# First batch's feed-forward in eight plain block products; the sums of weight blocks made during the second batch

## The chip, the cores and the metric

One core of a Trainium2 chip. The metric is the device time of one execution in microseconds (us); lower is better. The engines named below are PE (TensorE, matrix products), DVE (VectorE), ACT (ScalarE), POOL (GpSimd) and SP (the queue from which most DMAs are issued).

## The reference

Eight batches of attention over 576 positions (8 heads of 64, a window of 128 keys, a bias by distance), and behind it a feed-forward part with a maximum over three products:

```python
scores = scale * np.matmul(q, k.transpose(0, 1, 3, 2))
...
mask = (rel >= 0) & (rel < window)
scores = np.where(mask, scores + bias[None], -1000000000.0)
...
attn = attn / (np.sum(attn, axis=-1, keepdims=True) + 1e-09)
return np.matmul(attn, v).astype(np.float32)
...
h = np.maximum(np.maximum(x @ w1, x @ w2), x @ w3)
return (h @ w_out).astype(np.float32)
```

x has 4608 rows (8 batches of 576) of 512; w1, w2, w3 are 512x768, w_out is 768x512. The weights come as 64-bit floating-point numbers and are turned into 32-bit words on the chip.

## The kernel before

**Stages.** The program works in stages, one per batch of attention (20 steps each: 4 head pairs of 5 blocks of up to 128 queries). Stage 0 has only the attention of batch 0. Stage 1 has the attention of batch 1 and the feed-forward part of batch 0, stage 2 that of batch 2 beside the feed-forward part of batch 1, and so on; the last stage has only a feed-forward part. Each event (a step's scores, its transposes, a feed-forward unit) has a time number, and events are emitted in the order of these numbers. Within stages 0 and 1 a scheduler may then reorder the instructions of every engine by its own model; from an event early in stage 2 on, PE keeps the program's order (`fix`, `keep_in_program_order`). DVE, ACT, POOL and SP take their instructions in the order in which the scheduler placed them.

**The feed-forward part, seven products.** It is cut into 11 groups per batch: 9 of the first layer (3 blocks of hidden units for each of w1, w2, w3) and 2 of the output. Weights, inputs and outputs of a group are each seen as 2x2 blocks. Instead of the 8 block products of a 2x2 matrix product, each group has 7 "units" (a Strassen scheme in Winograd's form): unit k multiplies a sum of weight blocks by a sum of input blocks. `factors_x` makes the 7 input factors out of the attention's output `xk` (4 differences L397 and 7 splits), `factors_h` those of the hidden activations. Every float32 factor is split into a high part in PE's reduced format and a rest (ACT copy L393, subtraction on DVE or POOL L394), and a unit runs 3 matrix instructions per 128 rows of contraction: 6 in the first layer, 9 in the output layer, each 128x128 by 128x288 (`unit`, L518). The products land in three PSUM banks in turn; `put` (L467 to L484) takes them out, adds the partial sums and takes the maximum over the three weights; L527 copies a partial sum out with ACT.

**The weights.** `preparing` is a generator of 120 steps, 10 for each of 12 weight groups (9 of the first layer, 3 of w_out). `fetch` brings 64-bit words from HBM into two buffers; `convert` (L136 to L144: 2 ACT and 3 DVE operations of 128x512 per buffer) makes float32; `sums` (L158: 4 DVE operations of 128x256) makes the sums of blocks in place; `part` (L168 on ACT, L169 on DVE, 7 times 128x256) splits each of the seven factors into high part and rest. For a first-layer group, the split factors go into two ring tiles `wt0` (4 factors) and `wt1` (3 factors), two of each, and from there to HBM (`keep`, L171). w_out's factors stay in `ow`. The steps are taken two per attention step in stage 0 and two per unit in stage 1 (`weights`). From batch 1 on, the ring is filled from `keep` by DMAs issued on POOL's queue (`stream`, L221), as soon as PE has finished the group two before.

## Time and profile before

Median 839.39 us of 3 runs (836.74 to 843.86).

| what | value |
|---|---|
| span of the profiled execution (first to last instruction) | 837.3 us |
| its own time | not given apart from the span; the span lies inside the range of the runs, 2.1 us under their median |
| PE busy | 770.6 us (92%) |
| DVE, ACT, POOL busy | 560.9, 541.1, 303.7 us |
| mean granted TensorE clock | 0.963 |
| HBM read, written | 157.68 MB, 25.95 MB |
| first feed-forward product of batch 0 | 75.58 us |
| last output product of batch 0 | about 206 us |
| last output product of batch 1 | about 302 us |

The last three rows divide the span: 0 to 75.6 us is stage 0, 75.6 to 206 us is called stage 1 below and 206 to 302 us stage 2. A stage of the middle part (302 to 394 us, 394 to 486 us) takes 92 us. A busy share of an engine says little by itself here: what matters is which engine is full in which stage, and whether PE, which sets the pace from 206 us on, waits for it.

### The profile page before, as it was taken

The page shows a single profiled execution, that of the slowest core. Times are in us where ns is not written, and L with a number is a line of the kernel's source. Part 1 is how long each engine was busy: PE and PEld are TensorE (multiplying, and loading weights), DVE is VectorE, ACT ScalarE, POOL GpSimd, SP SyncE. Part 2 cuts the span into 40 slices and gives each one's busy share as a digit, 9 for nine tenths or more (in the row PEclk, how much of TensorE's full clock was granted, in tenths as well). Part 3 has the DMA queues.
Part 4 walks back from the last instruction along what each step waited for, and adds up shares of the span by engine and source line. Part 5 has one row for each costly group of instructions (what it writes and reads, how often), then busy time and mean ns, then how long its engine had stood idle before and what let it go on. Part 6 is the DMA issues. An engine that isn't in the chain of part 4 may idle for free.

```text
span 837.3 us, 17958 instructions
## 1 busy us (share of the span) xinstructions
PE 770.6 (92%) x6272; PEld 673.2 (80%) x6272; DVE 560.9 (67%) x1830; ACT 541.1 (65%) x1790; POOL 303.7 (36%) x544
## 2 busy tenths in 40 slices
PE   4876777799999999999999999999999999999888
PEld 2434666688988898889988998899888988899887
DVE  5788989987576846677566945675656846572552
ACT  6889888776657666576666755676557656652332
POOL 1221132423256415443255415441345315541431
PEclk9865988899999999999999999999999999999999
DMA  6652667674687747874588648873687557765851
GB/s 234 247 185 82 218 232 271 217 248 162 198 288 256 251 138 251 271 263 166 195 284 281 213 156 277 270 265 128 240 287 251 199 198 233 253 208 165 292 197 56
DMA packets 43401, 184.78 MB, mean 221 GB/s; under 512 B 4784, under 2 KB 13744, under 8 KB 34096
## 3 DMA queue, kind: packets, MB, share of 16 engines
q0 software_dynamic: 18144, 115.61, 41.7%
q1 hardware_dynamic: 25024, 67.97, 22.8%
q8 instruction: 49, 0.80, 0.4%
q14 instruction: 40, 0.33, 0.1%
q10 hardware_dynamic: 144, 0.07, 0.0%
HBM read 157.68 MB, written 25.95 MB: 219 GB/s over the span
## 4 chain that ended last, share of the span: by engine, by line
PE 63%; DVE 12%; issue 9%; POOL 7%; ACT 5%; DMA 3%; SPq 0%; POOLq 0%; DVEq 0%; ACTq 0%
PE ps_m L518 47%; PE ps_x L367 6%; PE ps_s L265 5%; POOL hs L394 5%; PE pt L327 4%; DMA wt<-keep 2%; DVE t L481 1%; DVE wt L169 1%; ACT p L299 1%; POOL pp L345 1%; DVE hq L482 1%; POOL pp L341 1%; DVE hs L144 1%; DVE xs L394 1%; DVE hs L158 1%
## 5 line engine op out<-in xcount | busy, mean ns | idle before, releaser
L518 PE MATMUL ps_m<-xs,wt 128*128 128x288 f32 x3024 | 441.0, 302 | 23.7 <-DVE hq L484 9.3
L518 PEld LDWEIGHTS ps_m<-xs,wt 128*128 128x128 f32 x3024 | 416.0, 192 | 35.8 <-DVE hq L484 11.5
L341 POOL TENSOR_SCALAR_AFFINE_SELECT pp<-pr 128x256 f32<-128x256 f32 (+1 forms) x128 | 54.5, 426 | 278.1 <-ACT pr L340 147.6
L527 ACT COPY t<-ps_m 128x288 f32<-128x288 f32 x264 | 102.1, 392 | 79.0 <-PE ps_m L518 78.9
L518 PE MATMUL ps_m<-hs,ow 128*128 128x288 f32 x1008 | 143.1, 298 | 4.1 <-POOL hs L394 2.4
L518 PEld LDWEIGHTS ps_m<-hs,ow 128*128 128x128 f32 x1008 | 136.0, 188 | 7.0 <-POOL hs L394 3.3
L299 ACT ACTIVATE p<-s,st 128x128 f32<-128x128 f32 (+1 forms) x320 | 127.0, 400 | 18.3 <-DVE st L295 17.4
L394 POOL TENSOR_TENSOR hs<-hq,hs 128x288 fp32r<-128x288 f32 x112 | 95.5, 861 | 100.0 <-ACT hs L393 99.9
L318 ACT ACTIVATE p<-p,st 128x128 f32<-128x128 f32 (+1 forms) x320 | 109.2, 395 | 16.1 <-DVE st L311 16.1
L221 POOL DMA_DIRECT2D wt<-keep x126 | 69.8, 554 | 124.3 <-PE ps_m L518 123.8
L481 DVE TENSOR_TENSOR t<-ps_m,t 128x288 f32<-128x288 f32 x144 | 64.6, 452 | 44.6 <-PE ps_m L518 28.5
L295 DVE CUSTOM_DVE_ANT_0 s<-ps_s,bias 128x128 f32<-128x128 f32 (+1 forms) x300 | 76.6, 281 | 18.5 <-PE ps_s L265 13.7
L367 PE MATMUL ps_x<-pp,v 128*64 128x256 f32 (+3 forms) x768 | 83.2, 341 | 5.2 <-POOL pp L341 4.4
L265 PE MATMUL ps_s<-qk 64*64 64x192 f32 (+1 forms) x1080 | 73.5, 345 | 12.3 <-DVE st L295 7.8
L283 DVE COPY_PREDICATED ps_s<-prev,ps_s 128x256 f32<-128x256 uint8 x120 | 50.7, 422 | 48.8 <-PE ps_s L265 47.4
L327 PE MATMUL pt<-ident,p 128*128 128x128 f32 (+1 forms) x320 | 63.6, 302 | 17.1 <-ACT p L318 15.6
L327 PEld LDWEIGHTS pt<-ident,p 128*128 128x128 f32 (+1 forms) x320 | 36.1, 147 | 49.8 <-ACT p L318 21.5
L367 PEld LDWEIGHTS ps_x<-pp,v 128*64 128x64 f32 (+1 forms) x768 | 46.2, 142 | 32.7 <-issue 10.3
L393 ACT CAST hs<-hq 128x288 fp32r<-128x288 f32 x120 | 49.5, 430 | 35.1 <-DVE hq L482 23.4
L482 DVE TENSOR_TENSOR hq<-t,hq 128x288 f32<-128x288 f32 x144 | 69.5, 486 | 2.8
L265 PEld LDWEIGHTS ps_s<-qk 64*64 64x64 f32 x1080 | 42.4, 141 | 30.6 <-issue 10.8
L340 ACT COPY pr<-pt 128x256 f32<-128x256 f32 x64 | 19.0, 322 | 72.4 <-PE pt L327 72.3
(56 smaller groups left out, 750.2 us busy)
## 6 DMA issues: line engine op xcount, KB each, us to landing
wt<-keep POOLq DMA_DIRECT2D x63, 1024.0 KB, 7.4
wt<-keep POOLq DMA_DIRECT2D x63, 768.0 KB, 4.8
qk<-in_qk SPq DMA_DIRECT2D x31, 576.0 KB, 6.0
hs<-in_w_all SPq DMA_DIRECT2D x24, 512.0 KB, 6.1
v<-in_v SPq DMA_DIRECT2D x32, 320.0 KB, 5.4
keep<-wt SPq DMA_DIRECT2D x9, 1024.0 KB, 4.3
outT<-t SPq DMA_DIRECT2D x64, 144.0 KB, 1.8
keep<-wt SPq DMA_DIRECT2D x9, 768.0 KB, 5.1
```

Source lines behind the costliest of these rows:

```text
L221: nc.gpsimd.dma_start(wts[n, a], keep[n % 9][a])
L265: pe(nc.tensor.matmul(ps[j][d:d + D, o:o + k1 - k0], lhsT=qkt[t][j * D:(j + 1) * D, 0, q0:q0 + D], rhs=qkt[t][j * D:(j + 1) * D, 1, k0:k1] ...
L295: nc.vector.tensor_tensor_reduce(out=s[:n], in0=ps[j][:n, P:2 * P], in1=(bias if i else bias0)[:n, 2 * hp + j, :], scale=-0.125, scalar=3. ...
L299: nc.scalar.activation(p[:n, j], s[:n], AF.Exp, bias=st[:n, 0, a, j:j + 1], scale=-1.0, accum_out=st[:n, 1, a, j:j + 1])
L318: nc.scalar.activation(p[:n, j], p[:n, j], AF.Copy, scale=st[:n, 2, a, j:j + 1])
L327: pe(nc.tensor.transpose(out=pt[:, a, j, :n], in_=p[:n, j], identity=ident[:n, :n]))
L367: pe(nc.tensor.matmul(x[j * D:(j + 1) * D, c:c + e - a], lhsT=vv[:n, i, j * D:(j + 1) * D], rhs=w[:n, j].rearrange("p a b -> p (a b)")[:, ...
L394: e.tensor_tensor(out=lo, in0=src, in1=hi.bitcast(F32), op=ALU.subtract)
L481: nc.vector.tensor_tensor(out=s, in0=ps, in1=e, op=ALU.add)
L482: nc.vector.tensor_tensor(out=h, in0=s, in1=h, op=ALU.max)
L518: pe(nc.tensor.matmul(ps, lhsT=lt, rhs=rt, start=i == 0 and k in (0, 1, 4), stop=i == len(pairs) - 1, skip_group_check=True,))
L527: nc.scalar.copy(out=e, in_=ps)
```

## The change

Batch 0 no longer uses the seven-product scheme. Its groups run in 8 plain block products (`plain_unit`: 4 output blocks, each the sum of two products that are accumulated in one PSUM bank). `plain_x` splits the 4 input blocks as they are, `plain_h` the 4 blocks of each hidden part; there are no differences to make, and `put` gets a finished block, so that it copies (ACT) or takes the maximum (DVE) and adds nothing.

The weights for this are the four blocks themselves: `part` now splits two blocks of 256 in one operation of 128x512. `convert` writes the float32 words densely, and SP sends them to HBM (`w32`). Three of the four split blocks are factors of the seven-product scheme too and go to `keep` at once. The 48 steps of this first pass are taken one per attention step in stage 0 and one per two units in stage 1. A second pass of 36 steps (`add`, `add_part`) makes the rest while batch 1's units run: for each group it reads the float32 words back, places the ring tiles for batch 1, loads the finished factors from `keep`, makes the four sums on DVE, splits them (one operation of 128x768 and one of 128x256 for a first-layer group, four of 128x256 for a group of w_out) and writes them to `keep`. All these DMAs are on SP's queue. A group of the second pass may start when PE's units of the group two before are emitted; w_out's three groups stand between groups 2 and 3. POOL's loads of `keep` begin with batch 2 instead of batch 1.

```diff
     def convert(g, j):
-        lw, hw = words(g, j)
+        both = raws[g, j].rearrange("p (n w) -> p n w", w=2)
+        lw, hw = both[:, :, 0], both[:, :, 1]
...
-        nc.vector.tensor_tensor(out=lf, in0=lf, in1=hw, op=ALU.mult)
...
+        out = raws[g, j][:, :DM].bitcast(F32)
+        nc.vector.tensor_tensor(out=out, in0=lf, in1=hw, op=ALU.mult)
+        nc.sync.dma_start(w32[g][:, j], out)
+
+    def halve(hi, lo, src):
+        nc.scalar.copy(out=hi, in_=src)
+        nc.vector.tensor_tensor(out=lo, in0=src, in1=hi.bitcast(F32), op=ALU.subtract)
...
+        halve(t[:, :, 0], t[:, :, 1], src.rearrange("p (i w) -> p i w", w=W))
+        for i in range(2):
+            plain[g, i, c] = t[:, i]
+            k = SLOT[i, c]
+            if k != 1:
+                nc.sync.dma_start(keep[g][k // 4][:, k % 4], t[:, i].bitcast(F32))
...
+    def add(g):
+        r = hs_p.tile([P, 2, 2 * W], F32, name="hs2", bufs=4)
+        q = sums[g] = hs_p.tile([P, 4, W], F32, name="hs2", bufs=4)
+        nc.sync.dma_start(r, w32[g])
...
+        if g < 9:
+            for a, ks in enumerate(((0,), (0, 2))):
+                place(9 + g, a)
+                for k in ks:
+                    nc.sync.dma_start(wts[9 + g, a][:, k].bitcast(F32), keep[g][a][:, k])
...
+    def add_part(g, a):
+        q = sums[g]
         if g < 9:
-            if k in (0, 4):
-                place(g, k // 4)
-            t = wts[g, k // 4][:, k % 4]
+            t, src = (wts[9 + g, 1][:, 1:2], q[:, 3:]) if a else (wts[9 + g, 0][:, 1:], q[:, :3])
+            halve(t[:, :, 0], t[:, :, 1], src)
+            if a:
+                nc.sync.dma_start(keep[g][1][:, 1:2], t.bitcast(F32))
+            else:
+                nc.sync.dma_start(keep[g][0][:, 1:], t.bitcast(F32))
...
-    g_order = [0, 1, 9, 10, 11, 2, 3, 4, 5, 6, 7, 8]
+        return (n - RING, 6 if a else 3) in used
+
+    A_ORDER = [0, 1, 2, 9, 10, 11, 3, 4, 5, 6, 7, 8]
+    B_ORDER = [0, 1, 2, 9, 10, 11, 3, 4, 5, 6, 7, 8]
...
-    streamed = 18
+    streamed = 36
...
+    def plain_unit(v):
...
+        weights(r % 2, 4 * (A_ORDER.index(g) + 1) if g < 9 else 48)
...
+        if c == 0:
+            part_of["plain"] = ps_m.tile([P, 512], F32, name=f"ps_m{(4 * g + o) % 3}")[:, :C]
+        ps = part_of["plain"]
+        for m, (lt, rt) in enumerate(pairs):
+            pe(nc.tensor.matmul(
+                ps, lhsT=lt, rhs=rt, start=m == 0 and c == 0, stop=m == len(pairs) - 1, skip_group_check=True,
+            ))
...
+        if c:
+            put(0, g, ij, ps, None, u)
...
+        if b == 1:
+            weights(k % 2, 48 + 3 * (B_ORDER.index(g) + 1) if g < 9 else STEPS)
...
     for s in range(1, n_steps + LAG_X):
-        at(s + 0.2, weights, 2)
+        at(s + 0.2, weights, 1)
```

DVE's instructions before, in stage 1 while batch 0's third group is multiplied (hs2_1120 and hs2_1122 hold the weights of first-layer group 4, wt0_1341 its factors, hq the hidden activations, ps_m a PSUM bank):

```order
L137 SCALAR_TENSOR_TENSOR hs2_1122<-hs2_1122 128x512
L158 TENSOR_TENSOR hs2_1120<-hs2_1120 128x256
L141 TENSOR_SCALAR hs2_1122<-hs2_1122 128x512
L481 TENSOR_TENSOR t_1328<-ps_m1_1321,t_1214 128x288
L144 TENSOR_TENSOR hs2_1122<-hs2_1122 128x512
L482 TENSOR_TENSOR hq_1016<-t_1328,hq_1016 128x288
L158 TENSOR_TENSOR hs2_1120<-hs2_1120,hs2_1122 128x256
L397 TENSOR_TENSOR t_1331<-hq_1000,hq_1016 128x288
L158 TENSOR_TENSOR hs2_1122<-hs2_1120 128x256
```

DVE's instructions now, at the same weight group (hs2_924 and hs2_926 hold it, wt0_1177 its four split blocks):

```order
L148 TENSOR_TENSOR hs2_926<-hs2_926 128x512
L544 TENSOR_TENSOR hq_1030<-ps_m1_1139,hq_1030 128x288
L357 TENSOR_SCALAR st_1057<-st_1057 128x4
L344 ISA s_1171,st_1170<-ps_s_105,bias_114 128x128
L344 ISA st_1170 128x1
L360 RECIPROCAL st_1057<-st_1057 128x4
L344 ISA s_1174,st_1170<-ps_s_105,bias_114 128x128
L344 ISA st_1170 128x1
L153 TENSOR_TENSOR wt0_1177<-hs2_924,wt0_1177 128x2x256
L544 TENSOR_TENSOR hq_940<-ps_m2_1161,hq_940 128x288
L153 TENSOR_TENSOR wt0_1177<-hs2_926,wt0_1177 128x2x256
L544 TENSOR_TENSOR hq_961<-ps_m0_1192,hq_961 128x288
```

The four sums and the pairs of addition and maximum are gone from this place; two wide subtractions and single maxima stand there, between the attention's operations (L344 to L360).

DVE's instructions now, in stage 2 while batch 1's second group of products leaves PSUM (hs2_2823 and hs2_2824 are words and sums of w_out's third group, ow its factors, wt1_2588 the ring tile of first-layer group 2). In the program before, this place has no weight work, only the additions and maxima of `put` and the attention's operations:

```order
L153 TENSOR_TENSOR ow5_123<-hs2_2809,ow5_123 128x256
L360 RECIPROCAL st_2556<-st_2556 64x2
L195 TENSOR_TENSOR hs2_2824<-hs2_2823 128x256 x2
L195 TENSOR_TENSOR hs2_2824<-hs2_2824,hs2_2823 128x256
L195 TENSOR_TENSOR hs2_2824<-hs2_2823,hs2_2824 128x256
L549 TENSOR_TENSOR t_2601<-ps_m1_2543,t_2581 128x288
L549 TENSOR_TENSOR t_2613<-ps_m2_2606,t_2539 128x288
L550 TENSOR_TENSOR hq_2482<-t_2601,hq_2482 128x288
L550 TENSOR_TENSOR hq_2491<-t_2613,hq_2491 128x288
L153 TENSOR_TENSOR wt1_2588<-hs2_2584,wt1_2588 128x256
L153 TENSOR_TENSOR ow1_119<-hs2_2824,ow1_119 128x256
L153 TENSOR_TENSOR ow2_120<-hs2_2824,ow2_120 128x256
```

The work of w_out's three groups and of first-layer groups 2 and 3 stands on DVE ahead of the factors that batch 1's fourth group of products needs.

SP's queue now, at the same place (w32 are the float32 words, keep the factors in HBM, v and qk the attention's inputs):

```order
L183 DMA hs2_2808<-w32_10_153 128x1024
L537 DMA outT<-t_2432 128x288
L190 DMA wt0_2586<-keep2_0_129 128x512
L183 DMA hs2_2823<-w32_11_154 128x1024
L288 DMA qk_2370<-in_qk 128x1152
L205 DMA keep2_0_129<-wt0_2586 128x1536
L190 DMA wt1_2588<-keep2_1_130 128x512 x2
L183 DMA hs2_2838<-w32_3_146 128x1024
L293 DMA v_2541<-in_v 128x640
```

Reads of words, loads and stores of factors, and the attention's loads share one queue here; before, it held only outT, qk and v.

More of the change, by code (lines that the diff above doesn't have):

```diff
@@ L119, in attention_maxout_kernel @@
     keep = [[dram.tile([P, e, 2, W], F32, name=f"keep{g}_{a}") for a, e in enumerate((4, 3))] for g in range(9)]
+    w32 = [dram.tile([P, 2, 2 * W], F32, name=f"w32_{g}") for g in range(NG)]
     wts = {}
@@ L189, in preparing @@
                 yield
-            sums(g)
-            yield
-            for k in range(7):
-                while g < 9 and not ahead(g, k // 4):
-                    yield True
-                part(g, k)
+            while 3 <= g < 9 and (g - 3, "plain") not in used:
+                yield True
+            for c in range(2):
+                part(g, c)
                 yield
             if n + 2 < NG:
-                fetch(g_order[n + 2])
+                fetch(A_ORDER[n + 2])
+        for g in B_ORDER:
+            while g < 2 and (8, "plain") not in used:
+                yield True
+            while 2 <= g < 9 and not ahead(9 + g, 1):
+                yield True
+            while g >= 9 and (10, "plain") not in used:
+                yield True
+            add(g)
+            yield
+            for a in range(2):
+                add_part(g, a)
+                yield
+    STEPS = 7 * NG
     prepared = 0
@@ L218, in stream @@
         n, a = divmod(streamed, 2)
-        if n < 9 * B and prepared == 120 and ahead(n, a):
+        if n < 9 * B and prepared == STEPS and ahead(n, a):
             place(n, a)
@@ L485, in put @@
         if w == 2:
-            factors_h(b, p, ij, when + 1)
+            if b:
+                factors_h(b, p, ij, when + 1)
+            else:
+                plain_h(p, ij, when + 1)
     part_of = {}
+    def plain_unit(v):
+        u = v * 77 / 88
+        while todo and todo[0][0] <= u:
+            _, what, args = todo.pop(0)
+            what(*args)
+        g, r = divmod(v, 8)
+        o, c = divmod(r, 2)
+        i, j = ij = ((0, 0), (0, 1), (1, 0), (1, 1))[o]
+        weights(r % 2, 4 * (A_ORDER.index(g) + 1) if g < 9 else 48)
+        if g < 9:
+            wt, x = plain[g, i, c], xs[0, 2 * c + j]
+            pairs = [
+                (wt[:, a, kt * P:(kt + 1) * P], x[:, e, kt]) for kt in range(2) for a, e in ((0, 1), (1, 0), (0, 0))
+            ]
+        else:
+            ms = slice((g - 9) * P, (g - 8) * P)
+            pairs = [
+                (plain[9 + p, i, c][:, a, ms], hs[0, 2 * c + j, p][:, e])
+                for p in range(3) for a, e in ((0, 1), (1, 0), (0, 0))
+            ]
+        if c == 0:
+            part_of["plain"] = ps_m.tile([P, 512], F32, name=f"ps_m{(4 * g + o) % 3}")[:, :C]
[4 more added lines that the diff above has]
+            ))
+        if r == 7:
+            used.add((g, "plain"))
+        if c:
+            put(0, g, ij, ps, None, u)
     def unit(u):
@@ L499, in unit @@
         b, g = divmod(n, 11)
+        if b == 0:
+            return
+        if b == 1:
+            weights(k % 2, 48 + 3 * (B_ORDER.index(g) + 1) if g < 9 else STEPS)
         if g < 9:
             at = b * 9 + g
[L502 to L503 removed]
             wt, x = wts[at, k // 4][:, k % 4], xs[b, k]
@@ L565, in attention_maxout_kernel @@
         if b == 0:
-            at(when, factors_x, 0, 0, 0)
+            at(when, plain_x)
+        if b == 0:
+            pace = (ready[1] - when) / 72
+            for y in range(88):
+                if y == 72:
+                    when = max(when, ready[1])
+                    at(when, factors_x, 1, 63, 1.2)
+                at(when, plain_unit, y)
+                when += pace if y < 72 else O_PACE
+            continue
         pace = (ready[b + 1] - when) / 63 if b + 1 < B else O_PACE
```

68 lines of the change are left out of this document (43 added, 25 removed).

## The prediction

> **What bounds the kernel now.** First I read the slices of the page, to see in which stage which engine is full:
>
> ```profile
> PE   4876777799999999999999999999999999999888
> DVE  5788989987576846677566945675656846572552
> ACT  6889888776657666576666755676557656652332
> PEclk9865988899999999999999999999999999999999
> ```
>
> Up to about the tenth slice (210 us) DVE and ACT are full and PE is not, at a reduced clock; from there PE is full. The table by stage says it in numbers (stage 1, stage 2, one middle stage, then the first two pieces of stage 1; the columns are busy us of PE, weight loads, DVE, ACT, POOL, then granted clock, DMA share, GB/s):
>
> ```profile
> 75.60:206.00 130.40, 108.26 (x780) 90.84 (x781) 117.60 (x357) 103.41 (x319) 37.87 (x57) 0.89 0.61 213
> 206.00:302.00 96.00, 94.31 (x825) 84.40 (x823) 64.80 (x216) 62.55 (x219) 40.11 (x73) 1.00 0.68 227
> 302.00:394.00 92.00, 90.46 (x786) 81.68 (x784) 59.42 (x202) 60.06 (x206) 37.51 (x69) 1.00 0.70 234
> 75.60:85.00 9.40, 7.64 (x36) 7.00 (x37) 8.70 (x21) 8.78 (x24) 0.05 (x1) 0.74 0.03 2
> 85.00:95.00 10.00, 6.32 (x42) 5.36 (x41) 9.82 (x35) 7.49 (x23) 1.50 (x2) 0.83 0.57 216
> ```
>
> Stage 1 does the same feed-forward work as a middle stage, yet takes 130.4 us instead of 92. DVE is busy in 90% of it (117.60 of 130.40), against 65% in the middle. What PE waits for is in its timeline of stage 1 (in brackets the wait and who ended it), which also has the stage's first and last products:
>
> ```profile
> 75.58 2.54 PE L518 MATMUL ps_m<-xs,wt 128*128 128x288 f32 x12 [0.31 <-DVE xs L394]
> 89.46 0.76 PE L265 MATMUL ps_s<-qk 64*64 64x192 f32 x12 [3.06 <-DVE st L295]
> 116.63 0.47 PE L327 MATMUL pt<-ident,p 128*128 128x128 f32 x1 [3.06 <-ACT p L318]
> 159.14 3.25 PE L518 MATMUL ps_m<-xs,wt 128*128 128x288 f32 x12 [3.42 <-ACT t L527]
> 167.94 2.17 PE L518 MATMUL ps_m<-xs,wt 128*128 128x288 f32 x12 [1.90 <-DVE hq L484]
> 202.58 3.60 PE L518 MATMUL ps_m<-hs,ow 128*128 128x288 f32 x25 [0.19 <-ACT t L527]
> ```
>
> PE waits for results from DVE and ACT, which are queued behind the weight work. From 206 us on, 535 us remain in which the order of work doesn't change; I leave them alone.
>
> **The change, stage by stage.** Durations on DVE and ACT, from the groups of 75 to 205 us (busy us, mean ns):
>
> ```profile
> L169 DVE TENSOR_TENSOR wt<-hs,wt 128x256 fp32r<-128x256 f32 x49 | 22.3, 473 | 3.8 <-ACT wt L168 3.6
> L168 ACT CAST wt<-hs 128x256 fp32r<-128x256 f32 x49 | 19.8, 424 | 4.4 <-DVE st L308 1.9 <-DVE hs L158 1.9 <-DVE hs L144 0.3
> L158 DVE TENSOR_TENSOR hs<-hs 128x256 f32<-128x256 f32 x21 | 8.9, 436 | 0.0
> L144 DVE TENSOR_TENSOR hs<-hs 128x512 f32<-128x512 f32 x14 | 9.7, 707 | 0.0
> L140 ACT ACTIVATE hs<-hs 128x512 int32<-128x512 f32 x14 | 9.6, 690 | 2.8 <-DVE hs L137 2.7
> L481 DVE TENSOR_TENSOR t<-ps_m,t 128x288 f32<-128x288 f32 x18 | 8.0, 447 | 1.5 <-PE ps_m L518 1.5
> L476 DVE TENSOR_TENSOR hq<-ps_m,hq 128x288 f32<-128x288 f32 x6 | 2.7, 450 | 1.2 <-PE ps_m L518 1.2
> ```
>
> In a full queue an operation costs less than its duration, since the next begins before it ends:
>
> ```profile
> 127.20 0.41 DVE L141 TENSOR_SCALAR hs<-hs 128x512 int32<-128x512 int32 x1
> 127.53 0.68 DVE L137 SCALAR_TENSOR_TENSOR hs<-hs 128x512 int32<-128x512 int32 x1
> 128.14 0.68 DVE L144 TENSOR_TENSOR hs<-hs 128x512 f32<-128x512 f32 x1
> ```
>
> 0.41 us costs 0.33 and 0.68 costs 0.61, so I take 0.07 off each: about 0.37 for 128x256 and 128x288, 0.63 for 128x512. No row has 128x768; by the step from 256 to 512 I estimate 0.90, and even twice the 512 form would add only 0.36 to each of seven.
>
> *Stage 0.* By the order, ACT splits 30 blocks of 128x256 there before, and now 6 of 128x512 and 10 of 128x256 (30 x 0.42 against 6 x 0.68 + 10 x 0.42: -4.3 us), and converts one weight group more (4 x 0.68 = +2.7). Net -1.6 on ACT; DVE loses some 7. ACT is the fuller one:
>
> ```profile
> 60.00:80.00 20.00, 12.08 (x72) 6.98 (x70) 16.73 (x58) 18.45 (x60) 5.06 (x10) 0.66 0.28 92
> ```
>
> 18.45 of 20, so I count ACT's: 75.6 becomes 74.0 (bounds 68.5, all of DVE's 7, and 76). The new writes of words on SP stand ahead of loads of q and v, but DMA here is 28% busy.
>
> *Stage 1, PE.* 504 matrix instructions become 576. One costs 0.132 us at full rate:
>
> ```profile
> 292.85 8.33 PE ps_m L518 x63
> L327 PE MATMUL pt<-ident,p 128*128 128x128 f32 (+1 forms) x44 | 10.9, 319 | 6.0 <-ACT p L318 6.0
> ```
>
> A middle stage is 92 us with 504 of them (66.6), so a batch of attention costs PE 25.4. Stage 1 holds 44 of the 40 transposes of a batch, 1.1 batches: 576 x 0.132 + 1.1 x 25.4 = 104 us if nothing stops PE. The eighth product thus costs 72 x 0.132 = 9.5 us of PE that nothing hides.
>
> *Stage 1, DVE.* Gone: 54 splits (x 0.40), 28 sums (x 0.37) and three conversion steps for two buffers (3.5), 35.5; the pairs L481 and L482 (36 x 0.38), 15 more additions (5.7), 12 differences of hidden blocks (5.0), and three differences and three splits of inputs (4.8), 29.2. Added: 12 wide and 2 narrow splits (8.3), the second pass for groups 0 and 1 (5.4), 18 more maxima and two splits (7.6). 117.6 - 64.7 + 21.3 = 74 us. In 109 us that is 68%, near the 65% at which the middle stage holds PE full. ACT comes to about 80 us (73%). So PE sets the pace, and I add what the start costs: clock 0.74 and 0.83 for the first 19.4 us lose 0.26 x 9.4 + 0.17 x 10 = 4 us, and 1 for waits. Stage 1: **109 us** instead of 130.4 (bounds 104, and 122 if half of today's 36 us above its own PE work of 504 x 0.132 + 28 = 94.5 stays).
>
> *Stage 2, DVE.* The ten other groups of the second pass: 7 x (4 x 0.37 + 0.90 + 0.37) + 3 x 8 x 0.37 = 28 us, on top of 64.80: 93 us. PE needs 94 to 96. DVE has held at most 90% over a stage (117.60 of 130.40); 93/0.90 = 103. **Stage 2: 103 us** instead of 96. I expect the loss at one place: the sums of w_out's groups and of group 3 stand ahead of the fourth group, about 18 to 20 us of DVE work more within two groups of products. The lower bound is 96, all of it hidden; the upper bound is in the rivals. DMA gets more too (words read back, factors stored), up to some 265 GB/s (estimated from sizes: per group of about 10 us 1.25 MB read back, 1 MB stored, 0.4 MB of q, k and v); the trace has held 363:
>
> ```profile
> 135.00:145.00 10.00, 5.35 (x35) 3.71 (x36) 10.00 (x31) 7.06 (x21) 2.09 (x3) 0.85 0.97 363
> hs<-in_w_all SPq DMA_DIRECT2D x24, 512.0 KB, 6.1
> ```
>
> A read of words lands in about 6 us like those of `in_w_all`, and is queued a group ahead.
>
> A weighing against the move: sums of two SBUF operands go to where POOL works more (40.11 of 96 us busy, against 37.87 of 130.4).
>
> ```profile
> L482 DVE TENSOR_TENSOR hq<-t,hq 128x288 f32<-128x288 f32 x144 | 69.5, 486 | 2.8
> L481 DVE TENSOR_TENSOR t<-ps_m,t 128x288 f32<-128x288 f32 x144 | 64.6, 452 | 44.6 <-PE ps_m L518 28.5 <-ACT t L527 11.1 <-ACT p L299 3.9
> L394 POOL TENSOR_TENSOR hs<-hq,hs 128x288 fp32r<-128x288 f32 x112 | 95.5, 861 | 100.0 <-ACT hs L393 99.9
> ```
>
> With two SBUF operands (L482) an operation takes 34 ns more than with one (L481): 66 of them, 2 us, within the rounding of 103. The Trainium skill ("SBUF — State Buffer", Who interferes with whom) says that a DVE operation with two SBUF inputs and a POOL operation that reads SBUF exclude each other for a whole instruction. The mean of 34 ns is far less than a whole instruction; the case in which it is not is the second rival.
>
> *Sum.* 74 + 109 + 103 = 286 against 302: -16 us. The span 837.3 becomes 821; the span lay 2 us below the median, so **823 us**.
>
> **The rivals.**
>
> The last rows are the loads of `keep` (KB each, us to landing) and one difference of hidden blocks on DVE (ns shortest, median, longest):
>
> ```profile
> wt<-keep POOLq DMA_DIRECT2D x63, 1024.0 KB, 7.4
> wt<-keep POOLq DMA_DIRECT2D x63, 768.0 KB, 4.8
> L397 DVE TENSOR_TENSOR hq<-hq x24: 442/642/950, 119.3 to 817.2; 128x288 f32<-128x288 f32 x24
> ```
>
> 1. *The turnaround of the ring* (slower). Now a ring tile is filled in stage 2 only after PE frees it: load from `keep`, ACT copy, DVE difference, all behind SP's and DVE's queues. Before, finished factors were loaded by POOL. From release to need is about one group, 96/11 = 9 us. If the seven groups 2 to 8 are late by 4.5 us each, stage 2 grows by 31 us, and this is the point where the kernel gets slower by over 1%: 16 + 8 of gain and margin plus the 7 already counted. At 5 us each: 74 + 109 + 131 = 314, **851 us**. For it: SP waits for PE's releases, in order, with stores of factors and q and v between. Against it: words are read a group ahead, and only pieces of 256 KB are loaded late (768 KB land in 4.8 us). Chance 0.12. The trace shows clock falling with such waits (the 0.83 and 0.85 above); the Trainium skill ("TensorE: Matmul & The Clock Gate", The HAM clock gate) has half rate after an idle window of about 3.4 us, which would add a little to each late group and no new case.
> 2. *POOL in DVE's way.* A DVE operation meets a POOL operation with the chance of POOL's share, 0.42, and waits half of 0.86 us: 0.18 us. 66 operations: 12 us, DVE 105, stage 2 at 90% 117 us: **837 us**. For it: single operations last up to 950 ns instead of 442. Against: that mean, and POOL loses its 18 loads in this stage. Chance 0.15.
> 3. *Stage 1 isn't freed.* Half of the waiting stays because the scheduler's order, and not DVE's load, makes PE wait: 122 us, **836 us**. For it: PE waits for attention steps too. Against: middle stages with the same kinds of waits lose nothing at 65%. Chance 0.12.
> 4. *All hidden.* Stage 1 at 105, stage 2 at 96: 275, **812 us**. For it: DVE has slack at stage 1's end. Chance 0.10.
>
> That the sums would not move at all is excluded by the order of instructions.
>
> **The numbers.** The forecast has 0.51, 815 to 831 us. A measurement here tells about 1% from no change: faster is under 831, slower over 848. Faster: 0.48 of the forecast, 0.10 of rival 4, and 0.05 of the lower ends of 2 and 3: 0.63. Slower: rival 1 and 0.01 of the others, 0.13. Same: 0.24. The range reaches from rival 4's middle to over rivals 2 and 3: 810 to 843; outside are most of rival 1 and the outer halves of the ends.
>
> **What would show it.** Right: first product of batch 0 near 74 us, its last near 183; DVE under 75% busy between them and clock near 1.00 after 95 us; in stage 2 DVE near 90% and one wait of PE of some 5 us ahead of the fourth group; last output product of batch 1 near 286 us; 535 us from there. Wrong: PE waits for L153 or loads of `keep` in every group of stage 2 (rival 1); L195 well over 500 ns (2); PE waits above 15 us in stage 1 (3). A change after stage 2 would break the forecast in all its cases.

## The result and the profile after

The changed kernel takes 817.11 us (median of 4 runs, 814.93 to 818.97), the kernel before beside it 840.25 us (836.74 to 843.86): a ratio of 0.973, with an interval of 0.969 to 0.977. Run twice more, beside the experiments below, it came to ratios of 0.978 (0.976 to 0.979) and 0.974 (0.972 to 0.977). The prediction said 823 (810 to 843), and faster with a chance of 0.63.

The slices of the changed kernel's page, to be held against those of the kernel before:

```profile
PE   4767998999889999999999999999999999999987
DVE  5777878479997756693757756694657746573552
ACT  6988888478776656676667656676667656552332
PEclk7776999999999999999999999999999999999999
```

PE is nearly full from the fifth slice (82 us) on, not only from the ninth (167 us), and at the full clock. DVE is full only once more, in slices 10 to 12 (184 to 245 us): this is where most of the second pass now runs.

For the table by stage I first looked up again where the last output product of each batch lies (timeline of PE: start, duration, then the group). Before:

```profile
202.58 5.05 PE L518 MATMUL ps_m<-hs,ow 128*128 128x288 f32 x36 [0.19 <-ACT t L527]
208.78 1.85 PE L518 MATMUL ps_m<-xs,wt 128*128 128x288 f32 x12
210.47 1.38 PE L518 MATMUL ps_m<-hs,ow 128*128 128x288 f32 x9
...
305.07 1.38 PE L518 MATMUL ps_m<-hs,ow 128*128 128x288 f32 x9
```

After:

```profile
181.04 2.66 PE L585 MATMUL ps_m<-hs,ow 128*128 128x288 f32 x18
...
285.59 1.38 PE L623 MATMUL ps_m<-hs,ow 128*128 128x288 f32 x9
```

In the kernel before, the last 9 output products (operands `hs`, `ow`) stand behind 12 products of the next batch (`xs`, `wt`) and end at 211.85 and 306.45 us, not at the 206 and 302 that the table ahead of the prediction has. (The 25 products at 202.58 us in the prediction are the part up to 206 us of the group of 36 above, which ends at 207.63.) In the changed kernel they end at 183.70 and 286.97. Cut at these ends, stages 0, 1 and 2 before are (busy us of PE, weight loads, DVE, ACT, POOL; granted clock, DMA share, GB/s):

```profile
0.00:75.60 75.60, 50.08 (x313) 24.39 (x313) 55.96 (x223) 62.42 (x212) 17.23 (x42) 0.78 0.59 207
75.60:211.85 136.25, 114.11 (x834) 96.23 (x835) 120.74 (x371) 106.14 (x331) 39.35 (x61) 0.89 0.59 208
211.85:306.45 94.60, 92.91 (x810) 82.97 (x810) 63.86 (x214) 62.54 (x221) 39.16 (x71) 1.00 0.70 234
```

and after:

```profile
0.00:74.60 74.60, 45.43 (x312) 22.50 (x312) 50.73 (x200) 61.17 (x205) 15.45 (x42) 0.73 0.72 248
74.60:183.70 109.10, 105.78 (x894) 96.17 (x895) 79.87 (x258) 82.04 (x254) 24.89 (x46) 0.97 0.68 223
183.70:286.97 103.27, 97.10 (x822) 84.87 (x822) 87.67 (x276) 75.50 (x251) 33.48 (x57) 1.00 0.76 255
```

Stage 0 gains 1.0 us and stage 1 gains 27.2; stage 2 loses 8.7. Of the last two, 1.6 us (12 x 0.132) only changed sides: the first 12 products of batch 1 lay in stage 1 before and lie in stage 2 now (822 matrix instructions there instead of 810). From there to the end of the span it is 530.9 us before and 530.3 after. Together that is 20.0 us less, the difference of the spans (837.3 and 817.3).

In stage 1 PE is busy in 105.78 of 109.10 us. Its waits there are these three lines (us in all, times, longest), where before there were many, up to 6.0 us in sum on one line. The first ended at 74.60 us, where the stage begins, so only 3.3 us lie inside it:

```profile
PE ps_m L585 <- DVE xs L443: 2.6, 1, 2.6
PE ps_s L314 <- DVE st L344: 2.6, 2, 2.3
PE ps_m L585 <- ACT hq L546: 0.7, 1, 0.7
```

In stage 2 PE's eight waits are short and lie apart, 5.9 us in all. Three of them (timeline, in brackets the wait; the first is one unit into the fourth group, the second one unit into the fifth):

```profile
209.63 3.46 PE L623 MATMUL ps_m<-xs,wt 128*128 128x288 f32 x24 [0.56 <-DVE t L549]
220.16 3.53 PE L623 MATMUL ps_m<-xs,wt 128*128 128x288 f32 x24 [1.84 <-DVE hq L552]
237.60 1.06 PE L623 MATMUL ps_m<-xs,wt 128*128 128x288 f32 x6 [1.04 <-ACT t L632]
```

### The profile page after: what moved, and what is told of

Its sections match the earlier page's. It is cut to its first block, busy times and chain, and to the rows that moved or that the text cites. A ratio compares the mean times of both kernels' runs of the same rounds, so it can differ in the third digit from the quotient of the medians.

```text
span 817.3 us, 18140 instructions
## 1 busy us (share of the span) xinstructions
PE 761.5 (93%) x6344; PEld 673.1 (82%) x6344; DVE 538.2 (66%) x1756; ACT 528.7 (65%) x1736; POOL 281.8 (34%) x515
## 4 chain that ended last, share of the span: by engine, by line
PE 61%; DVE 9%; issue 9%; DMA 8%; POOL 6%; ACT 6%; SPq 0%; POOLq 0%; DVEq 0%; ACTq 0%
PE ps_m L623 41%; PE ps_x L416 6%; PE ps_m L585 6%; PE ps_s L314 5%; POOL hs L443 4%; PE pt L376 4%; DMA hs<-w 2%; DMA wt<-keep 2%; DMA hs<-in_w_all 2%; ACT p L348 2%; DMA w<-hs 1%; DVE hs L195 1%; DVE wt L153 1%; ACT p L367 1%; DVE t L549 1%
## 5 line engine op out<-in xcount | busy, mean ns | idle before, releaser
L632 ACT COPY t<-ps_m 128x288 f32<-128x288 f32 x231 | 89.4, 392 | 75.3 <-PE ps_m L623 75.3
L623 PE MATMUL ps_m<-hs,ow 128*128 128x288 f32 x882 | 124.5, 298 | 3.0 <-POOL hs L443 1.4
L443 POOL TENSOR_TENSOR hs<-hq,hs 128x288 fp32r<-128x288 f32 x106 | 90.6, 862 | 102.6 <-ACT hs L442 102.4
L623 PEld LDWEIGHTS ps_m<-hs,ow 128*128 128x128 f32 x882 | 118.8, 189 | 5.1 <-POOL hs L443 2.1
L270 POOL DMA_DIRECT2D wt<-keep x108 | 59.8, 554 | 106.1 <-PE ps_m L623 104.5
L344 DVE CUSTOM_DVE_ANT_0 s<-ps_s,bias 128x128 f32<-128x128 f32 (+1 forms) x300 | 76.7, 281 | 17.8 <-PE ps_s L314 10.9
L416 PE MATMUL ps_x<-pp,v 128*64 128x256 f32 (+3 forms) x768 | 80.8, 338 | 4.7 <-POOL pp L390 4.5
L549 DVE TENSOR_TENSOR t<-ps_m,t 128x288 f32<-128x288 f32 x126 | 56.3, 452 | 37.4 <-PE ps_m L623 21.5
L314 PE MATMUL ps_s<-qk 64*64 64x192 f32 (+1 forms) x1080 | 69.6, 335 | 9.5 <-DMA qk<-in_qk 4.9
L376 PE MATMUL pt<-ident,p 128*128 128x128 f32 (+1 forms) x320 | 59.1, 295 | 12.4 <-ACT p L367 8.5
```

The costliest lines, as they stand in the source:

```text
L270: nc.gpsimd.dma_start(wts[n, a], keep[n % 9][a])
L314: pe(nc.tensor.matmul(ps[j][d:d + D, o:o + k1 - k0], lhsT=qkt[t][j * D:(j + 1) * D, 0, q0:q0 + D], rhs=qkt[t][j * D:(j + 1) * D, 1, k0:k1] ...
L344: nc.vector.tensor_tensor_reduce(out=s[:n], in0=ps[j][:n, P:2 * P], in1=(bias if i else bias0)[:n, 2 * hp + j, :], scale=-0.125, scalar=3. ...
L376: pe(nc.tensor.transpose(out=pt[:, a, j, :n], in_=p[:n, j], identity=ident[:n, :n]))
L416: pe(nc.tensor.matmul(x[j * D:(j + 1) * D, c:c + e - a], lhsT=vv[:n, i, j * D:(j + 1) * D], rhs=w[:n, j].rearrange("p a b -> p (a b)")[:, ...
L443: e.tensor_tensor(out=lo, in0=src, in1=hi.bitcast(F32), op=ALU.subtract)
```

## The experiments

For each profiled execution the first product, the ends of batch 0 and batch 1 (last output product, as above) and the span, with the median of all runs (us). All kernels stand beside runs of the kernel before on the same chip, whose medians were 838.2 to 840.3.

| kernel | first product | end of batch 0 | end of batch 1 | span | median | ratio to before (interval) |
|---|---|---|---|---|---|---|
| before | 75.6 | 211.9 | 306.5 | 837.3 | 840.3 | 1 |
| changed | 74.6 | 183.7 | 287.0 | 817.3 | 817.1 | 0.973 (0.969 to 0.977) |
| changed, 2nd | 73.9 | 181.4 | 282.8 | 817.0 | 820.0 | 0.978 (0.976 to 0.979) |
| changed, 3rd | 75.4 | 183.1 | 283.4 | 815.1 | 817.3 | 0.974 (0.972 to 0.977) |
| no second pass | 77.2 | 182.9 | 278.5 | 810.9 | 812.0 | 0.967 (0.964 to 0.970) |
| sums twice | 74.4 | 181.2 | 290.9 | 821.1 | 825.5 | 0.986 (0.980 to 0.992) |
| seven, light weights | 72.8 | 186.3 | 281.0 | 814.3 | 815.0 | 0.970 (0.966 to 0.974) |
| eight, sums first | 82.7 | 194.6 | 290.3 | 824.7 | 824.3 | 0.982 (0.979 to 0.985) |
| words by POOL | 75.2 | 181.3 | 283.8 | 814.0 | 817.2 | 0.976 (0.973 to 0.979) |
| w_out spread | 75.2 | 182.5 | 286.6 | 819.8 | 822.3 | 0.980 (0.977 to 0.982) |
| splits on POOL | 75.1 | 182.7 | 291.2 | 822.5 | 822.9 | 0.981 (0.979 to 0.983) |
| half in stage 0 | 69.4 | 177.8 | 279.2 | 810.1 | 816.1 | 0.974 (0.972 to 0.977) |
| 3/4 in stage 0 | 73.2 | 181.8 | 282.6 | 815.3 | 817.0 | 0.975 (0.973 to 0.977) |
| half, words by POOL | 69.7 | 178.7 | 283.7 | 814.5 | 815.0 | 0.972 (0.970 to 0.974) |

The same program's own executions differ: stage 2 of the changed kernel lasts 103.3, 101.4 and 100.4 us in its three profiles, and its medians by chip differ by 0.4%. The rest behind batch 1 lasts 530.3, 534.2 and 531.7 us in them, though the order of work there is the same. Differences of under 3 us between its variants are read with that in mind.

Two questions stood open. Where does the gain come from: from relieving DVE, which was full in stage 1 (my theory), or from the simpler products as such? And what makes stage 2 longer: the load of DVE, of which about 90% is the most that it can hold (my theory), or waits for transfers and bursts in single places (the rival)?

The expectations of the next four runs count the changed kernel's stages up to 183.6 and 282.5 us. The second of these lies near the end of the last long group of products and not at the last product, so stage 2 is 98.9 us there, with 85.46 us of DVE, for the 103.3 and 87.67 of the table by stage.

### Without the second pass

```diff
-            if k != 1:
-                nc.sync.dma_start(keep[g][k // 4][:, k % 4], t[:, i].bitcast(F32))
+            for k in {0: (0, 2), 1: (1, 3), 4: (4, 5), 6: (6,)}[k]:
+                nc.sync.dma_start(keep[g][k // 4][:, k % 4], t[:, i].bitcast(F32))
...
-        for g in B_ORDER:
+        for g in ():
```

> The changed kernel without its second pass: no words are read back, no sums are made in stage 2, and from batch 1 on the factors that need sums are replaced by copies of plain split blocks (so batches 1 to 7 compute something else, with the same number and shapes of products). POOL loads keep from batch 1 on, as in the kernel before. Theory (DVE's extra work in stage 2 costs the 3 us by which stage 2 is longer than before): DVE in stage 2 falls from 85 to about 58 us, stage 2 from 98.9 to 95 or 96, stage 1 stays near 108, total about 813. Rival (the second pass is hidden entirely, and stage 2 is longer for another reason, such as a shorter lead of the inputs): stage 2 stays at 98 to 99, total 816 to 818.

Measured: 812.0 us. This kernel leaves out the sums, so its batches 1 to 7 compute other values. Stages 1 and 2, in the columns used above:

```profile
77.23:182.86 105.63, 104.16 (x894) 94.58 (x895) 74.68 (x242) 80.96 (x253) 24.93 (x50) 0.98 0.78 273
182.86:278.47 95.61, 94.80 (x822) 84.61 (x822) 63.05 (x214) 64.39 (x225) 38.65 (x71) 1.00 0.68 231
```

The theory holds and its rival falls: stage 2 is back at 95.6 us with PE busy in 94.80 of it. The second pass costs DVE 87.67 - 63.05 = 24.6 us in stage 2, and the kernel 5.1 us by the medians (4.7 to 7.7 us of stage 2, by the three profiles of the changed kernel). In the first profile 5.4 of the 7.7 us are waits of PE (6.2 us for 0.8), and 2.3 are that PE is busy longer with the same 822 instructions (97.10 us for 94.80); why it is, is not shown. The edit also takes 11.1 us off ACT and the pass's reads and stores off the queues. The next run adds to DVE alone.

### The sums made twice

```diff
             (s3, a00, a10, ALU.subtract),
-        ):
+        ) * 2:
```

> The changed kernel with the four sums of each weight group in the second pass made twice (same values): about 40 sums more on DVE in stage 2, at 0.36 us each some 14 us, which takes DVE from 85.5 to about 100 us. Theory of the prediction (DVE can't hold more than 90% over a stage): stage 2 becomes 100/0.90 = 111 us, total about 829. Rival A (what stage 2 loses comes from waits for the reads of words on SP, not from DVE's load; DVE can be filled to nearly 100%): stage 2 about 101 to 103, total 819 to 821. Rival B (DVE has slack for it): no change, 817.

Measured: 825.5 us. Stage 2:

```profile
181.15:290.90 109.75, 98.74 (x822) 86.85 (x822) 98.44 (x319) 77.84 (x257) 35.85 (x58) 0.97 0.73 245
```

With 10.8 us more on DVE, stage 2 is 6.5 to 9.4 us longer, so DVE's work does set the loss: rival B (817) falls, and so does rival A's cause, since no read was added. The size lies between the theory and rival A. The total is 3.5 us under the theory's 829 and 4.5 over rival A's 821. By the expectation's count, up to the end of the last long group, stage 2 is 104.5 us (181.15 to 285.62), for the theory's 111 and rival A's 101 to 103. DVE is busy in 95.77 us of that, 92%, so a limit of 90% is not shown. Most of the added time is one wait at the place that the prediction had named for the changed kernel, the start of the fourth group (timeline of PE), and the clock behind it (stretches of 2 us):

```profile
213.35 0.61 PE L623 MATMUL ps_m<-xs,wt 128*128 128x288 f32 x1 [6.07 <-ACT wt L152]
```

```profile
207.00:209.00 2.00, 0.29 (x3) 0.05 (x1) 2.00 (x7) 1.06 (x5) 2.00 (x5) 1.00 0.16 66
209.00:211.00 2.00, 0.00 (x0) 0.00 (x0) 2.00 (x7) 0.41 (x1) 0.11 (x1) 1.00 0.00 0
211.00:213.00 2.00, 0.00 (x0) 0.00 (x0) 2.00 (x7) 0.87 (x2) 0.35 (x1) 0.77 0.33 131
213.00:215.00 2.00, 0.95 (x2) 0.63 (x3) 2.00 (x8) 1.12 (x4) 1.74 (x2) 0.50 0.75 209
215.00:217.00 2.00, 2.00 (x10) 2.00 (x10) 2.00 (x6) 1.14 (x5) 1.20 (x2) 0.50 0.92 379
217.00:219.00 2.00, 2.00 (x10) 2.00 (x10) 2.00 (x9) 0.78 (x2) 0.00 (x0) 0.53 0.34 95
219.00:221.00 2.00, 2.00 (x17) 1.76 (x17) 2.00 (x6) 1.96 (x6) 0.85 (x1) 1.00 0.90 323
```

DVE is full throughout (2.00 of 2.00); PE waits 6.07 us, and comes back at a granted clock of 0.50 until about 219 us, with 20 products in the 4.0 us from 215 to 219, where 30 fit at 0.132 us each. So this wait cost more than itself. (The Trainium skill, "TensorE: Matmul & The Clock Gate", The HAM clock gate, has half rate after an idle window of about 3.4 us; this trace agrees for the 6.07 us. In the changed kernel's second profile a clock of 0.50 came behind 1.84 us too, as the last section shows.)

### Which half of the change gains: products or weight work

Seven products as before, weight work as light as in the new first pass:

```diff
-        src = blocks(g)[k]
+        src = blocks(g)[7 if k == 1 else k]
...
+        if k in (2, 3, 5):
+            if g < 9 and k == 3:
+                for x in (0, 2):
+                    nc.sync.dma_start(keep[g][0][:, x:x + 2], wts[g, 0][:, :2].bitcast(F32))
+            return
...
-            sums(g)
...
-            wt, x = wts[at, k // 4][:, k % 4], xs[b, k]
+            f = {2: 0, 3: 1, 5: 4}.get(k, k)
+            wt, x = wts[at, f // 4][:, f % 4], xs[b, k]
```

> The kernel before (seven products in every batch), with the weight work made as light as in the new first pass: no sums, and four splits of 128x256 per group in place of seven; the other three factors are copies of plain blocks, so the output is another one, with all products, additions and maxima as before. DVE in stage 1 loses 28 sums and 21 splits, about 19 of its 117.6 us, ACT 9 of 103. Theory (stage 1 is set by the load of DVE at about 90%): stage 1 falls from 130.4 to 107 to 111, total 816 to 821: the weight work alone is worth what the whole change is worth, and the plain products pay for themselves only. Rival (the additions and input differences of the seven products hold stage 1 up as well): stage 1 stays above 118, total above 827.

Eight products, with the sums still made in the first pass:

```diff
-            if n + 2 < NG:
-                fetch(A_ORDER[n + 2])
-        for g in B_ORDER:
...
             add(g)
             yield
...
                 add_part(g, a)
                 yield
+            if n + 2 < NG:
+                fetch(A_ORDER[n + 2])
...
-    streamed = 36
+    streamed = 18
...
-        weights(r % 2, 4 * (A_ORDER.index(g) + 1) if g < 9 else 48)
+        weights(1 if r else 0, 7 * (A_ORDER.index(g) + 1) if g < 9 else STEPS)
...
-        at(s + 0.2, weights, 1)
+        at(s + 0.2, weights, 1 + s % 2)
```

> Batch 0 in eight plain products as in the changed kernel, but the sums and their splits are still made in stages 0 and 1, from the words in SBUF, with no words in HBM and no second pass; the result is the reference's. DVE's work in stage 1 is then the changed kernel's 79.9 us, less 5 for the second pass of two groups, plus about 9 groups of 2.8 to 3 us: some 100 to 102 us. Theory (90% of DVE's load sets stage 1): stage 1 about 113, stage 2 back at 95 to 96, total 817 to 821, so that moving the sums to stage 2 is worth little by itself. Rival A (the sums in stage 1 are what costs, whatever the products): stage 1 125 to 130, total 830 to 836. Rival B (the products are what matters): stage 1 109, stage 2 96, total 813 to 815.

Measured: 815.0 and 824.3 us. The first of these kernels leaves out the sums and so computes other values. Stage 1 of the first, then stage 1 and stage 2 of the second:

```profile
72.83:186.32 113.49, 106.00 (x834) 90.05 (x835) 99.22 (x316) 96.11 (x306) 38.62 (x61) 0.97 0.70 247
```

```profile
82.73:194.60 111.87, 107.45 (x894) 93.83 (x895) 95.89 (x294) 92.11 (x274) 30.78 (x50) 1.00 0.68 239
194.60:290.27 95.67, 94.84 (x822) 84.61 (x822) 63.07 (x214) 64.62 (x225) 38.69 (x71) 1.00 0.70 239
```

Medians by products and by where the sums are made:

| | sums in the first pass | sums in the second pass | no sums at all |
|---|---|---|---|
| seven products in batch 0 | 840.0 (the kernel before) | not possible: its products need the sums | 815.0 |
| eight plain products in batch 0 | 824.3 | 817.1 | 812.0 |

With seven products the sums and their splits cost 25 us; with eight in the same place 12, of which 5.5 lie ahead of the first product (82.7 for 77.2); moved to stage 2, 5. And the plain products alone are worth 15.7 us while DVE carries the sums (840.0 to 824.3), 3 us where it does not (815.0 to 812.0), though they add 9.5 us of PE. So it is one effect with two sources: both take work off DVE and ACT, and the more of it is gone, the less the next piece brings. Stage 1 is 136.3 us with 120.7 us of DVE, 113.5 with 99.2, 111.9 with 95.9, 109.1 with 79.9, 105.6 with 74.7: it falls one for one down to 99, and by 7.9 us over the next 24.5, towards the 104 to 107 that PE is busy there. (The last steps are near the spread: with 80 us of DVE stage 1 is 107.5 to 109.1 in the changed kernel's three profiles, and 106.0 with the words by POOL.) The theory for the seven products held: stage 1 is 113.5 us, or 109.3 up to the end of its last long group at 182.1, nearer to the expectation's count, for 107 to 111; the total is 1 us under its range. For the eight it missed the place: stage 1 came as expected (112, for 113), but the total was 3 us over the expected range, because part of the sums' steps is taken in stage 0 (last lines of the edit), and the first product comes 8 us later, at 82.7. I had counted nothing for stage 0. Its rivals A (830 to 836) and B (813 to 815) both fall: products and sums each matter.

### Where in stage 2 the second pass costs its 5 us

The changed kernel stood beside three variants in these runs.

> The changed kernel once more, beside the three variants of it that follow, which differ from it by less than 1%. Every theory: 816 to 818.

The reads of the words on another queue:

```diff
-        nc.sync.dma_start(r, w32[g])
+        nc.gpsimd.dma_start(r, w32[g])
```

> The changed kernel, with the reads of the float32 words issued on POOL's queue in place of SP's; nothing else. In stage 2 DVE stands idle for 4.7 us on these reads, which on SP are queued behind loads that wait for PE. Theory 1 (these idle stretches are what DVE then lacks, and PE waits for): idle of DVE before the sums falls below 1 us, total 2 to 3 us less, 814 to 815. Theory 2 (the load of DVE alone sets the loss of stage 2, and an idle stretch is caught up with): no change, 816.5 to 818. Theory 3 (POOL is busy with its own work when the reads should start, so they start later): 819 to 822.

The second pass in another order:

```diff
-    B_ORDER = [0, 1, 2, 9, 10, 11, 3, 4, 5, 6, 7, 8]
+    B_ORDER = [0, 1, 2, 3, 9, 4, 5, 10, 6, 7, 11, 8]
```

> The changed kernel, with the second pass in another order: w_out's three groups stand between first-layer groups 3 and 4, 5 and 6, 7 and 8, no longer all three ahead of group 3. The amount of work is the same. Theory 1 (the loss comes from local bursts, in which DVE has more to do than the stretch allows: DVE is 99% busy from 193 to 203 and 100% from 213 to 223 us): with the burst gone 2 to 4 us less, 813 to 815. Theory 2 (the sum of DVE's work over the stage sets the loss): no change, 816.5 to 818; DVE full somewhat later instead.

Measured: 820.0 for the changed kernel, 2 us above what was expected of it, 817.2 and 822.3 for the two; the last is above the ranges of both its theories. Against the kernel before, the intervals of the three overlap (0.976 to 0.979, 0.973 to 0.979, 0.977 to 0.982), so neither gain that I expected is shown. DVE's idle time on the reads, 4.7 us in the first profile of the changed kernel, is 2.6 and 3.0 in its second and third with nothing changed, and 2.5 with POOL's queue; stage 2 lasts 102.6 us there, inside the 100.4 to 103.3 of the changed kernel. With w_out spread DVE waits only 0.5 us for reads, and stage 2 still lasts 104.1 us. So neither the wait for the reads nor the burst of w_out's groups is shown to be what stage 2 loses. The load of DVE over the whole stage fits both. One wait is common to these runs: 1.84 us, one unit into the fifth group, ended by DVE's L552, in all three profiles of the changed kernel and with the words by POOL (2.35 us with w_out spread), and there is none at that place without the second pass. No run here removed that wait alone, so what it is worth stays open.

The splits moved to POOL:

```diff
-    def halve(hi, lo, src):
+    def halve(hi, lo, src, on=None):
         nc.scalar.copy(out=hi, in_=src)
-        nc.vector.tensor_tensor(out=lo, in0=src, in1=hi.bitcast(F32), op=ALU.subtract)
+        (on or nc.vector).tensor_tensor(out=lo, in0=src, in1=hi.bitcast(F32), op=ALU.subtract)
...
-            halve(t[:, :, 0], t[:, :, 1], src)
+            halve(t[:, :, 0], t[:, :, 1], src, nc.gpsimd)
```

> The changed kernel, with the subtractions of the second pass's splits of first-layer groups (one of 128x768 and one of 128x256 per group) on POOL in place of DVE. It takes 10.8 us of duration, about 9.5 of queue time, off DVE in stage 2 and gives POOL, which is 33 of 103 us busy there, some 20 us more. Theory 1 (DVE's load sets the loss; it grows by 6.5 us for 10.8 us more on DVE, by the run with the sums made twice): stage 2 5 us shorter, total 812 to 814. Theory 2 (POOL's longer operations are in DVE's way or come too late for the products: a 128x768 subtraction should last some 2.3 us there): DVE's operations with two operands in SBUF get longer by over 50 ns in the mean or PE waits for the stored factors, total 816 to 821.

Measured: 822.9 us, 0.981 against 0.978 for the changed kernel beside it. Stage 2:

```profile
182.74:291.15 108.41, 99.50 (x822) 87.77 (x822) 88.65 (x262) 75.51 (x251) 52.23 (x71) 0.97 0.74 244
```

Theory 2 holds in its first half, with a total 2 us over its range. DVE has 14 operations fewer, which had 10.8 us, and is busy 88.65 us instead of 87.67: all of it came back in longer operations. The three groups with both operands in SBUF, L550 and the two of L195, have 7.0 us of it (12.5, 10.7 and 9.0 us for 9.0, 7.8 and 8.4). A group of L195, then two forms of the same size, one with both operands in SBUF (L550) and one with an operand in PSUM (L552; ns shortest, median, longest):

```profile
L195 DVE TENSOR_TENSOR hs<-hs,hs x18: 407/422/2049, 184.3 to 252.9; 128x256 f32<-128x256 f32 x18
L550 DVE TENSOR_TENSOR hq<-t,hq x18: 447/462/1591, 197.0 to 267.2; 128x288 f32<-128x288 f32 x18
L552 DVE TENSOR_TENSOR hq<-ps_m,t x9: 443/450/458, 186.4 to 249.0; 128x288 f32<-128x288 f32 x9
```

and two of the long ones on DVE, with POOL's rows for the same times:

```profile
211.16 1.38 DVE L550 TENSOR_TENSOR hq<-t,hq 128x288 f32<-128x288 f32 x1
...
236.29 1.59 DVE L550 TENSOR_TENSOR hq<-t,hq 128x288 f32<-128x288 f32 x1
```

```profile
210.39 1.83 POOL L153 TENSOR_TENSOR wt<-hs,wt 128x768 fp32r<-128x768 f32 x1
...
234.83 2.74 POOL L153 TENSOR_TENSOR wt<-hs,wt 128x256 fp32r<-128x256 f32 x2 [3.12 <-ACT wt L152]
```

DVE's operation ends at 212.54, 0.32 us after POOL's at 212.22; the other at 237.88, 0.31 after 237.57. Both last three times the usual 0.45 us and end just behind POOL's. Of L552, with an operand in PSUM, none is longer than 458 ns. So the second rival's mechanism is at work here. In the changed kernel, with POOL busy 33 us instead of 52, it costs little (2.8 us, worked out below).

### Stage 0, and the combination

Since stage 1 now has room on DVE and the run with the sums first showed stage 0 to be set by the weight work, I moved weight steps from stage 0 to stage 1.

```diff
-        at(s + 0.2, weights, 1)
+        at(s + 0.2, weights, s % 2 if s <= 20 else 1)
```

> The changed kernel, with the first pass of the weights taken one step per two attention steps in stage 0, in place of one per step; the ten steps left out there are made in stage 1, at the places where the products call for them. The work is the same. In the changed kernel ACT is busy in 61 of stage 0's 74.6 us and DVE in 51; ten steps are about 14 us of ACT and 17 of DVE. In the run with the sums in the first pass, stage 1 had 95.9 us of DVE in 111.9 us, against 79.9 in 109.1 (or 107.5 in the second run): about +3 us for 16. Theory 1 (stage 0 is set by ACT and DVE, and stage 1 has room for some 16 us of DVE): first product at 65 to 67, stage 1 110 to 113, total 812 to 815. Theory 2 (stage 0 is set by the attention's own chain of steps, not by the weight work beside it): first product at 72 to 74, stage 1 110 to 113, total 820 to 824.

```diff
-        at(s + 0.2, weights, 1)
+        at(s + 0.2, weights, int(s % 4 > 0) if s <= 20 else 1)
```

> The same with three steps of the weights per four attention steps in stage 0: five steps, about 7 us of ACT and 8 of DVE, are moved to stage 1. Theory 1: first product at 70, stage 1 109 to 111, total 813 to 816. Theory 2: first product at 74, total 818 to 821.

Measured: 816.1 and 817.0, first products at 69.4 and 73.2. With half the steps stage 0 and stage 1 are:

```profile
0.00:69.44 69.44, 49.53 (x312) 24.57 (x313) 38.78 (x175) 53.36 (x185) 15.20 (x42) 0.75 0.62 209
69.44:177.83 108.39, 106.38 (x894) 95.18 (x895) 92.30 (x284) 90.46 (x274) 29.25 (x46) 0.98 0.78 262
```

The first product comes 5 us earlier (I expected 8 to 10), and stage 1 is no longer with 92 us of DVE than with 80 (both theories had 110 to 113). So the weight work does delay the first product, though less than its own time. Theory 2 of the half falls on both numbers, and theory 1 is missed by 2 us in the first product and by 1 us in the total. With three quarters the first product is nearer theory 2's 74, and the total lies between the two. These runs had no changed kernel on the same chip; against the kernel before, the three intervals (0.972 to 0.977, 0.973 to 0.977, and 0.969 to 0.979 over the changed kernel's three) overlap. Then with the reads on POOL's queue besides, beside the changed kernel once more:

> The changed kernel with both edits that did not make it slower: half the weight steps in stage 0, and the reads of the words on POOL's queue. Theory 1 (both are worth what their medians showed: some 4 and 3 us, added): 5 to 7 us under the changed kernel run beside it. Theory 2 (the gain of stage 0 is real, since the first product comes 5 us earlier, and that of the reads is spread of the runs): 3 to 4 us under it. Theory 3 (both are spread): within 1.5 us.

> The changed kernel once more, on the same chip as the combination. All theories: 816 to 821.

Measured: 815.0 against 817.3, ratios to before of 0.9719 (0.9697 to 0.9741) and 0.9742 (0.9720 to 0.9765). Of the 5.7 us by which its first product is earlier, 4.4 are left at the end of batch 0 and none at the end of batch 1, where its profiled stage 2 took 105.0 us. The two are 2.3 us apart with intervals that overlap, so theory 1's 5 to 7 us did not come, theory 2's 3 to 4 are not shown, and theory 3 is not excluded. It is not settled that this version beats the changed kernel; both beat the kernel before.

## Why the prediction was right, point by point

- **Faster, and why**: right. Stage 1 was held up by work on DVE and ACT, and is now set by PE. The five stage 1 times beside DVE's load above go together, and the run with seven products and light weights shows that it is the load, not the form of the products.
- **Stage 0, 74.0 us**: measured 74.6 (73.9 and 75.4 in the other profiles). The time fits, but its working, ACT's 1.6 us less taken one for one, is not shown: the three lie 0.2 to 1.7 us under a single profile of the kernel before, and half the weight steps, with 7.8 us of ACT and 12.0 of DVE less in stage 0, moved the first product by only 5.2 us.
- **Stage 1, 109 us**: measured 109.1, then 107.5 and 107.7. PE's own work was put at 104, it was busy 105.8. DVE was put at 74 us and was 79.9, ACT at 80 and was 82.0; 73% of DVE still held PE full. The eighth product's 9.5 us is paid in full and still leaves a gain.
- **Stage 2, 103 us**: measured 103.3 (101.4 and 100.4 in the other profiles), but the two factors were each off, in opposite directions, and that they met at 103 is luck. DVE was put at 93 us and had 87.7 (the second pass takes 24.6, not 28), and its share was put at 0.90 and was 0.85. The share is no constant: it was 0.85 to 0.87 in the three profiles and 0.90 with the sums twice. Nor did the loss come in the form forecast, one wait of some 5 us ahead of the fourth group: the nearest wait was 0.56, and the loss lies in eight waits of 0.2 to 1.84 us and in products that take longer. The forecast place is right for a load of 10.8 us more, where it came as 6.07.
- **The sum**: 823 for 817.1; the term that was mis-sized is the rest of 535 us behind stage 2. It was counted from 302 us, where I took the last output product of batch 1 to be. The last one ends at 306.45, so the rest is 530.9, and it stayed within its spread (530.3; 534.2 and 531.7 in the other profiles). With this, the same steps give 74 + 109 + 103 + 530.9 = 817, and 819 with the 2 us to the median. The same mistake made stage 1 before look like 130.4 us where it was 136.3, so the gain there was set too low. 286 us for the end of batch 1 was near as a time (287.0, then 282.8 and 283.4), and wrong as a difference.
- **Rival 1, the ring**: did not come. None of PE's waits in stage 2 names a load of `keep`, one of 0.9 us names the ring's split (L153), and the longest of all is 1.84 us. The run with twice the sums shows its beginning: there a group's ring tile, waiting for DVE and then ACT, was late by 6 us.
- **Rival 2, POOL in the way**: rightly put low in chance here, but the argument against it was wrong. I held a mean of 34 ns to speak against an exclusion for a whole instruction. A mean cannot: most operations met nothing, a few waited whole. In the changed kernel's stage 2 the median of L550 is 452 ns and its longest 1062:

```profile
L550 DVE TENSOR_TENSOR hq<-t,hq x18: 450/452/1062, 196.8 to 262.9; 128x288 f32<-128x288 f32 x18
L195 DVE TENSOR_TENSOR hs<-hs x18: 397/418/1022, 183.9 to 250.9; 128x256 f32<-128x256 f32 x18
L195 DVE TENSOR_TENSOR hs<-hs,hs x18: 409/415/775, 184.5 to 251.9; 128x256 f32<-128x256 f32 x18
L195 DVE TENSOR_TENSOR hs<-hs 128x256 f32<-128x256 f32 x18 | 8.4, 495 | 4.7 <-DMA hs<-w 4.7
L195 DVE TENSOR_TENSOR hs<-hs,hs 128x256 f32<-128x256 f32 x18 | 7.8, 435 | 0.1
L550 DVE TENSOR_TENSOR hq<-t,hq 128x288 f32<-128x288 f32 x18 | 9.0, 510 | 0.1
```

  By mean less median, 18 x (77 + 20 + 58) ns = 2.8 us of DVE in these three groups, not the 12 of the rival. With POOL busy 52 instead of 33 us, such collisions gave back most of the 10.8 us that were taken off DVE.
- **Rival 3, stage 1 not freed**: excluded by PE's waits inside the stage, 3.3 us in all. **Rival 4, all hidden, 812**: not reached. It is the kernel without the second pass in both stages (105.6 and 95.6 us for its 105 and 96); that the totals agree to the microsecond (812.0) is partly luck, since that kernel's first product came at 77.2 us and not at 74.

What is shown: the load of the weight work and of the partial sums in stage 1 as the cause of the gain, and the second pass as the cause of what stage 2 gives back; for stage 2 the run with the sums twice, which adds sums to DVE alone (98.44 us for 87.67), shows that DVE's work sets it. Argued only: that in stage 1 it is DVE rather than ACT, since every run that took work from one took it from the other too (for DVE speaks that ACT was busy in 78% of stage 1 before, 106.14 of 136.25, and in 85% of the shorter stage 1 with light weights); and that stage 2 is set by the load over the stage rather than by any one wait, of which the two runs that were to find one showed none.

## What to carry to other kernels

When an engine is full in one stage and has room in the next, moving its work there is worth the difference of the two slopes: here 21.5 us of DVE, with 10.0 us of ACT that go with them, cost 22.8 us in a stage where DVE was nearly full (120.74 of 136.25 us; seven products, with and without the sums), and 24.6 us of DVE cost 5.1 in one that PE sets. Read the end of a stage at the last instruction of its kind, not at the last long group of them, because every later boundary and the rest inherit the error. And judge a collision by the shortest, median and longest duration of a form, since a mean hides a few operations that waited whole behind many that did not.
